# One fused attention and feed-forward kernel: when w_out's prepared tiles are stored, how long tiles rest, and which sums are kept

## The chip, the cores and the metric

The kernel runs on one core of a Trainium2 chip. The metric is the time of one execution on the device in microseconds; three executions of a kernel are summed up by their median. The profile is of one further execution and has a span of its own, from the first to the last instruction.

## The reference

```python
def _attn_ref(q, k, v):                       # q, k, v: (8, 12, 448, 64)
    scale = 1.0 / np.sqrt(q.shape[-1])
    scores = scale * np.matmul(q, k.transpose(0, 1, 3, 2)) - np.log(S)
    attn = 1.0 / (1.0 + np.exp(-scores))
    return np.matmul(attn, v)
...
def _moe_ref(x, w_in, w_out):                 # x: (3584, 768), w_in: (768, 2048), w_out: (2048, 768)
    h = x @ w_in
    g = np.maximum(0.01 * h, h)
    return g @ w_out
...
    x = attn_out.transpose(0, 2, 1, 3).reshape(B * S, H * D)
    return _moe_ref(x=x, **moe_kwargs)
```

All arrays are float32. The kernel multiplies each float32 as a high and a low part: every product of two tiles is three matmuls (high by high, high weight by low, low weight by high).

## The kernel before, in words

The work falls into three stages, one after the other on TensorE. **Attention** works through 48 pairs of heads. **The first product** (matmuls that write tiles named f) is x by w_in, in 4 rounds `p` of 20 block products, each in two halves: 160 steps called slots, of 12 matmuls of 448 columns each. **The second product** (matmuls that write tiles named a, and e for the last) is g by w_out, in 104 slots of 18 matmuls. Both products use fewer block products than a plain 4 by 4 blocking would, by a fast scheme with sums: blocks of weights and of inputs are added and subtracted first (`SUMS2` for the inputs and `STEPS2` for the weights of the second product), multiplied (`PRODUCTS2`), and the results added up.

The order on every engine is the order of the code: each engine's queue takes its instructions in that order. `slot()` emits one slot: the chores that were put down for it with `at(slot, rank, ...)` or `later(slots, ...)`, by rank, and the matmuls. SyncE (SP) issues nearly all transfers and also waits in order: a transfer whose data or room is not ready holds up those behind it.

**Preparation.** The generator `prep()` makes the weights on VectorE (DVE). It takes a unit u of w_in or w_out (12 units of w_out), decodes the packed words in two or three pieces into a tile wd (five instructions a piece), and makes the sums. For w_out that is `second()`: ten steps of `STEPS2`, most into a tile ws, some into free blocks of wd itself. Then both tiles are stored in memory (t2d, "t" in the trace), from where the second product's weights w are loaded. wd and ws of w_out take turns in one pool of two buffers, so wd always gets the same buffer back. Before the next unit's wd is begun, `prep()` waits until `now` has passed `free`, which is `HOLD` slots after the decoding of the last one ended; `PAUSE` means that no preparation is emitted in that slot. Otherwise the loop over `items1` emits as much preparation after a slot as the planned share of 2.42 us allows. The first unit of w_out is prepared at the end of the attention, the other eleven during the first product.

**Tiles.** `grab()` gives one of up to 28 tiles of 128 by 896 floats, the one that has been free longest; `drop(t, n)` gives it back for slot `now + n`. During the first product 16 of them exist; 6 more ("o") take the room of the preparation's pool after its end, and 6 ("j") come near the end. The results h of the first product are stored (g) by `save1`; sums of them that the second product needs (`MADE`, tiles h_m) are made by `made2` and stored too. The second product loads g tiles ahead; `LIMITS` says up to how many held tiles it may start a load early. `Streamed` weights ws are loaded from ts into three rotating tiles for the last products of a round. `Weights` loads the second product's weights, the first 12 (`FIRST`) before it begins, into buffers that the first product's weights leave.

The line behind an instruction in the profile is that of the recording helper (L159) nearly everywhere, so groups are told apart by tile names.

Of the kernel before, what the change touches and what calls it, by code (L numbers as in the profile page):

```python
# [21 lines left out]
ROOM = 1.7, 2.2, 2.1, 0.7, 0.2  # L22
SHARE = 0.95
SLOT = 2.42
CAST, SOON, HOLD = 3, 2, 3
PAUSE = 1
FULL = range(33, 37)
IDLE = 7
# [2 lines left out]
TILES, MORE, LAST, JOIN = 13, 3, 6, 6  # L31
RESULTS = 8
ROTS = 3
EARLY, FIRST, SOON2 = 12, 12, (2, 5)
COSTS = {"low": 0.95, "sum": 1.0, "cast": 0.85, "read": 1.5}
CAP, CAP_EARLY = 3.4, 0.8
GAP, LEAD, FAR2 = 8, 3, 5
LIMITS = (4, 27), (0, 22), (-3, 14), (-9, 10), (-99, 0)


X_ORDER = 1, 0, 2
# [28 lines left out]


RAW = "00", "01", "30", "31", "10", "11", "20", "21"
MADE = ("m1", "m2"), ("m5",), ("m1", "m2"), ("m3", "m4", "m5")


SUMS2 = {
# [7 lines left out]


PRODUCTS2 = (
# [7 lines left out]


BLOCKS2 = "02", "00", "01", "03", "10", "11", "12", "13", "s0", "s1", "s12", "s14", "s15"
MORE2 = "s2", "s3", "s4", "s5", "s6", "s7", "s8", "s9", "s10", "s11", "s13", "s16", "s17"
FORMS2 = BLOCKS2 + MORE2
STEPS2 = (
# [5 lines left out]


def part(i):
# [14 lines left out]
def attn_ffn_kernel(ctx: ExitStack, tc: tile.TileContext, qk, v, w_in, w_out, out):  # L122
# [21 lines left out]
    NQ = B // 2  # L144
# [52 lines left out]
    def later(slots, *fns, first=False):  # L197
        at(now + slots, 0 if first else 5, *fns)
# [13 lines left out]

    left, right = ExitStack(), ExitStack()

    prepared = set()

    class Wide:

# [178 lines left out]
    def second(u, w):  # L397


        kt, mt = divmod(u, 3)  # L400
        to = t2d[kt // 2][:, :, kt % 2, mt]
        s = block(F32, (len(MORE2), P), f"ws1_{u}")

        def of(x, y):
            names, t = (BLOCKS2, w) if x in BLOCKS2 else (MORE2, s)
            return two(t, names.index(x), names.index(y))

        for how, o, x, y in STEPS2:
            {"+": add, "-": sub, "n": minus}[how](*(of(z[0], z[-1]) for z in (o, x, y)))
            yield  # L410
        later(1, lambda: dma(out=to[:, :len(BLOCKS2)], in_=w), lambda: dma(out=to[:, len(BLOCKS2):], in_=s))

    def prep():

        count, size = (3, 2), 4 * P
        pieces = [(m, k) for m, (w, _) in enumerate(units) for k in range(count[w])]
        raws, free = [], 0

        def load():
            at = len(raws)
            if at == len(pieces):
                return
            m, k = pieces[at]
            w, u = units[m]
            third = w == 0 and at % 3 == 2
            raw = block(I32, (size, 2), f"wr{w}_{u}_{k}", (wr3, "wr3", 2 * size, 1) if third else (pp, "wr", 2 * size, 2))
            dma(out=raw.rearrange("p m t -> p (m t)"), in_=(w_in, w_out)[w][u][:, k * size:(k + 1) * size].bitcast(I32))
            raws.append((raw, now))  # L430

        for _ in range(3):
            load()
        yield
        for at, (m, k) in enumerate(pieces):
            w, u = units[m]
            if k == 0:
                while now < free:
                    yield PAUSE
                dec = block(F32, ((12, len(BLOCKS2))[w], P), f"wd{w}_{u}")  # L440
            while len(raws) <= at or now < raws[at][1] + SOON:
                yield PAUSE
            raw = raws[at][0]
            low, high = raw[:, :, 0], raw[:, :, 1]
            tf = dec.rearrange("p b m -> p (b m)")[:, k * size:(k + 1) * size]
            t = tf.bitcast(I32)
            vec_s(out=t, in0=high, scalar1=0x7FFFFFFF, scalar2=None, op0=ALU.bitwise_and)
            yield
            vec_s(out=tf, in0=tf, scalar1=W_LEAST, scalar2=W_MOST, op0=ALU.max, op1=ALU.min)
            yield  # L450
            vec_s(out=t, in0=t, scalar1=5, scalar2=2, op0=ALU.logical_shift_left, op1=ALU.logical_shift_right)
            yield
            vec_st(out=t, in0=high, scalar=-0x40000000, in1=t, op0=ALU.bitwise_and, op1=ALU.bitwise_or)
            yield
            vec_st(out=t, in0=low, scalar=29, in1=t, op0=ALU.logical_shift_right, op1=ALU.bitwise_or)
            yield
            if at != count[0] * NU - 1:
                later(1, load)
            if k < count[w] - 1:
                continue  # L460
            if w:
                free = now + 1 + HOLD
            while w and (0, NU - 1) not in prepared:
                yield PAUSE
            yield from (firsts, second)[w](u, dec)
            if w:
                prepared.add((w, u))
# [337 lines left out]
    def full(p, o, jj):  # L805

        got = complete.setdefault((p, jj), [])
        got.append(o)
        t = outs1[p, o, jj]
        at(now + 2, 8, lambda: save1(p, jj, o, t, True))  # L810
        todo = [(x, SUMS2[x][0], *(y[0] + str(int(y[1]) % 2) for y in SUMS2[x][1:])) for x in MADE[p]]
        for x in todo:
            if o in x[2:] and set(x[2:]) <= set(got):
                at(now + 1, 6, lambda x=x: made2(p, jj, *x))
        users = [set(x[2:]) for x in todo]
        for y in got:
            if (p, y, jj) not in over and all(z <= set(got) for z in users if y in z):
                over.add((p, y, jj))
                at(now + 2, 9, lambda t=outs1[p, y, jj]: drop(t, 2))

    def made2(p, jj, x, how, a, b):
        t = grab(f"h_{p}_{x}_{jj}", F32)
# [182 lines left out]
    w2 = [Weights(k) for k in range(LEN)]  # L1005
    for k, x in enumerate(w2):
        if k < FIRST:
            prepared_by(when(NQ - 1, 3 * (k // 4) + 3) + k % 4, x, 0)
        else:
            at(START + k - 9, 6, x.load)  # L1010
            at(START + k - 6, 1.6, x.high)
            at(START + lows[k], 1.7, x.low)

    used = 0.0
    for n, item in enumerate(items1):
        if n == len(items1) * (NQ - 1) // NQ:
            assert next(preps, 0) == 0
            right.close()
            shift(ctx, "pad5", 192, "right")
            tiles(ctx, "o", "right", LAST)  # L1020
# [16 lines left out]
    for tag, n in (("z0", 1), ("a1", 3), ("a0", 3), ("z1", 1)):  # L1037
        acc2[tag] = banks(f"ps_{tag}", {tag: (1, n)}, end)

    free = [(0, n) for n in range(RESULTS)]  # L1040
    outs, accs = {}, {}

    def result(o):
        place = min(free)
        free.remove(place)
        n = place[1]
        if n < ROTS:
            t = rot.tile([P, 2, NU, P], F32, tag=f"rot{n}", name=f"o_{o}").rearrange("p a b c -> p (a b c)")[:, :3 * S]
# [10 lines left out]
    def store(q, o):  # L1059
        t, n = outs.pop(o)  # L1060
        dma(out=place2(q, o).rearrange("m p s -> p m s"), in_=t)
        free.append((now + 3, n))

    def read(q, i):
        acc = accs[i % 2][:, :, :S]
# [91 lines left out]
```

## Time and profile before

| | us |
|---|---|
| median of 3 runs | 1053.4 (1053.33 to 1053.59) |
| the profiled execution | 1052.52 |
| its span | 1050.7 |
| TensorE matmuls busy | 1017.9 (97%) |
| VectorE busy | 851.2 (81%) |
| ScalarE busy | 585.1 (56%) |
| mean rate of the transfers | 280 GB/s |

The profiled execution lasted 1.8 us longer than its span. Busy time of TensorE overlaps in part and is not a measure of use; its idle time is.

### The profile page before, as it was taken

The page shows a single profiled execution, that of the slowest core. Times are in us where ns is not written, and L with a number is a line of the kernel's source. Part 1 is how long each engine was busy: PE and PEld are TensorE (multiplying, and loading weights), DVE is VectorE, ACT ScalarE, POOL GpSimd, SP SyncE. Part 2 cuts the span into 40 slices and gives each one's busy share as a digit, 9 for nine tenths or more (in the row PEclk, how much of TensorE's full clock was granted, in tenths as well). Part 3 has the DMA queues.
Part 4 walks back from the last instruction along what each step waited for, and adds up shares of the span by engine and source line. Part 5 has one row for each costly group of instructions (what it writes and reads, how often), then busy time and mean ns, then how long its engine had stood idle before and what let it go on. Part 6 is the DMA issues. An engine that isn't in the chain of part 4 may idle for free.

```text
span 1050.7 us, 15193 instructions
## 1 busy us (share of the span) xinstructions
PE 1017.9 (97%) x5642; PEld 848.2 (81%) x5642; DVE 851.2 (81%) x1116; ACT 585.1 (56%) x710; POOL 0.3 (0%) x5
## 2 busy tenths in 40 slices
PE   9999999999899979999999999699999999999998
PEld 5555555457898968988889999599999999999997
DVE  5888889876998588787776585579998899899886
ACT  6888888885544433454435664357444446645431
POOL 0000000000000000000000000000000000000000
PEclk9999999999999989999999999899999999999999
DMA  8899999988967978898879758997756798785632
GB/s 318 271 330 378 317 368 303 384 286 302 352 245 250 362 249 288 257 333 273 286 217 336 283 191 317 349 319 258 253 172 243 246 377 317 269 280 149 229 132 105
DMA packets 142745, 294.08 MB, mean 280 GB/s; under 512 B 11216, under 2 KB 71760, under 8 KB 142672
## 3 DMA queue, kind: packets, MB, share of 16 engines
q1 hardware_dynamic: 141808, 292.32, 80.3%
q8 instruction: 44, 0.72, 0.3%
q10 hardware_dynamic: 864, 0.80, 0.2%
q14 instruction: 29, 0.24, 0.1%
HBM read 189.79 MB, written 103.28 MB: 279 GB/s over the span
## 4 chain that ended last, share of the span: by engine, by line
PE 81%; DVE 8%; DMA 7%; issue 2%; SPq 1%; ACT 1%; ACTq 0%; DVEq 0%
PE a L159 35%; PE f L159 22%; PE pv L159 12%; PE sc L159 11%; DVE wd L159 3%; DMA t<-wd 3%; DMA g<-h 2%; DVE ws L159 2%; DVE xl L159 1%; SPq L159 1%; DVE h L159 1%; DMA ws<-ts 1%; DMA xd<-x_s 1%; ACT h L159 0%; DMA g<-g 0%
## 5 line engine op out<-in xcount | busy, mean ns | idle before, releaser
L159 PE MATMUL a<-gh,w 128*128 128x448 f32 x1224 | 344.7, 363 | 6.8 <-ACT h L159 6.8
L159 PE MATMUL f<-xh,w 128*128 128x448 f32 x960 | 274.8, 366 | 5.6 <-DVE h L159 3.4
L159 PEld LDWEIGHTS a<-gh,w 128*128 128x128 f32 x1224 | 230.6, 188 | 24.4 <-ACT h L159 7.2
L159 PEld LDWEIGHTS f<-xh,w 128*128 128x128 f32 x960 | 181.9, 190 | 22.1 <-DVE h L159 3.6
L159 PE MATMUL a<-gl,w 128*128 128x448 f32 x516 | 188.0, 364 | 0.0
L159 PE MATMUL f<-xl,w 128*128 128x448 f32 x480 | 176.0, 367 | 12.0 <-DVE xl L159 12.0
L159 DVE TENSOR_TENSOR h<-h,f 128x896 f32<-128x896 f32 x88 | 95.3, 1084 | 40.0 <-PE f L159 39.9
L159 ACT CAST gh<-g 128x896 fp32r<-128x896 f32 x68 | 64.0, 941 | 107.4 <-DVE g L159 78.7
L159 ACT ACTIVATE s<-sc 128x896 f32<-128x896 f32 x144 | 119.7, 957 | 3.6 <-PE sc L159 3.6
L159 ACT COPY h<-f 128x896 f32<-128x896 f32 x56 | 50.1, 909 | 118.6 <-PE f L159 91.2
L159 PE MATMUL pv<-s,v 128*64 128x448 f32 x576 | 113.8, 543 | 0.0
L159 PEld LDWEIGHTS f<-xl,w 128*128 128x128 f32 x480 | 91.1, 190 | 19.2 <-DVE xl L159 13.4
L159 DVE TENSOR_TENSOR w<-w 128x768 fp32r<-128x768 f32 x112 | 104.3, 953 | 0.1
L159 PEld LDWEIGHTS a<-gl,w 128*128 128x128 f32 x516 | 97.5, 189 | 5.3
L159 PEld LDWEIGHTS sc<-qks 64*128 64x128 f32 x876 | 80.4, 187 | 23.1 <-issue 16.9
L159 PE MATMUL sc<-qks 64*128 64x448 f32 (+1 forms) x876 | 95.3, 368 | 0.2 <-ACT qks L159 0.2
L159 PE MATMUL f<-xh,ws 128*128 128x448 f32 x320 | 91.5, 364 | 3.8 <-DVE h L159 2.0
L159 ACT CAST w<-w 128x768 fp32r<-128x768 f32 x112 | 92.8, 832 | 2.6 <-DMA w<-t 2.6
L159 PEld LDWEIGHTS pv<-s,v 128*64 128x64 f32 x576 | 39.0, 137 | 63.3 <-issue 54.3
L159 DVE TENSOR_TENSOR xl<-xl,xh 128x896 fp32r<-128x896 f32 x64 | 69.5, 1086 | 18.6 <-ACT xh L159 18.6
L159 ACT ACTIVATE h<-h 128x896 f32<-128x896 f32 x56 | 53.2, 952 | 52.3 <-DVE h L159 52.0
L159 DVE TENSOR_TENSOR qks<-qk,qks 128x832 fp32r<-128x832 f32 (+3 forms) x51 | 49.2, 971 | 36.9 <-ACT qks L159 35.5
(82 smaller groups left out, 1113.8 us busy)
## 6 DMA issues: line engine op xcount, KB each, us to landing
w<-t SPq DMA_DIRECT2D x112, 384.0 KB, 4.6
g<-g SPq DMA_DIRECT2D x76, 448.0 KB, 5.5
xl<-xd SPq DMA_DIRECT2D x64, 448.0 KB, 5.6
g<-h SPq DMA_DIRECT2D x64, 448.0 KB, 5.8
qk<-in_qk SPq DMA_DIRECT2D x46, 448.0 KB, 6.1
xd<-x_s SPq DMA_DIRECT2D x36, 448.0 KB, 7.0
xd<-x SPq DMA_DIRECT2D x28, 448.0 KB, 6.3
g_m<-g SPq DMA_DIRECT2D x28, 448.0 KB, 5.4
```

The source lines that it names most:

```text
L159: return lambda *args, **kw: tc.keep_in_program_order(issue(*args, **kw))
```

## The change

For w_out, the steps of `STEPS2` that write into wd come first, and wd is stored one slot after the last of them; ws is stored at the end as before. `free` now has a slot for each of the two tiles, five slots after the slot in which the store was put down (`now + 1 + HOLD`, with `HOLD` 4), and both the next wd and the next ws wait for theirs. The end of the preparation may come 12 slots later (`JOINT`: 28 slots before the end of `items1` in place of 40), and the 6 "o" tiles come then. The loads of the second product's first 12 weights move from slots 126 to 141 to slots 136 to 152. Tiles whose results were stored rest 3 slots in place of 2 (`drop(t, 3)`). `SUMS2` is another set of sums for the same products: rounds 0 and 2 still make and store two sums, round 1 one, and round 3 one in place of three. `LIMITS` is lower by 1 or 2 tiles. The tables `STEPS2`, `BLOCKS2`, `MORE2` and `PRODUCTS2` are written for the new sums; their counts (10 steps of the same widths, 26 products) are the same.

```diff
-CAST, SOON, HOLD = 3, 2, 3
+CAST, SOON, HOLD = 3, 2, 4
...
-EARLY, FIRST, SOON2 = 12, 12, (2, 5)
+EARLY, FIRST, SOON2, JOINT = 12, 12, (2, 5), 28
...
-LIMITS = (4, 27), (0, 22), (-3, 14), (-9, 10), (-99, 0)
+LIMITS = (4, 26), (0, 20), (-3, 12), (-9, 8), (-99, 0)
...
-MADE = ("m1", "m2"), ("m5",), ("m1", "m2"), ("m3", "m4", "m5")
+MADE = ("m1", "m4"), ("m5",), ("m1", "m4"), ("m5",)
...
-BLOCKS2 = "02", "00", "01", "03", "10", "11", "12", "13", "s0", "s1", "s12", "s14", "s15"
+BLOCKS2 = "02", "00", "01", "03", "10", "11", "12", "13", "s0", "s1", "s2", "s3", "s4"
...
+        while now < free["s"]:
+            yield PAUSE
         s = block(F32, (len(MORE2), P), f"ws1_{u}")
...
-        for how, o, x, y in STEPS2:
+        for n, (how, o, x, y) in enumerate(STEPS2):
             {"+": add, "-": sub, "n": minus}[how](*(of(z[0], z[-1]) for z in (o, x, y)))
+            if o[0] in BLOCKS2 and STEPS2[n + 1][1][0] in MORE2:
+                later(1, lambda: dma(out=to[:, :len(BLOCKS2)], in_=w))
+                free["w"] = now + 1 + HOLD
             yield
-        later(1, lambda: dma(out=to[:, :len(BLOCKS2)], in_=w), lambda: dma(out=to[:, len(BLOCKS2):], in_=s))
+        later(1, lambda: dma(out=to[:, len(BLOCKS2):], in_=s))
+        free["s"] = now + 1 + HOLD
...
-                while now < free:
+                while w and now < free["w"]:
                     yield PAUSE
...
-            if w:
-                free = now + 1 + HOLD
...
-                at(now + 2, 9, lambda t=outs1[p, y, jj]: drop(t, 2))
+                at(now + 2, 9, lambda t=outs1[p, y, jj]: drop(t, 3))
...
-            prepared_by(when(NQ - 1, 3 * (k // 4) + 3) + k % 4, x, 0)
+            prepared_by(START - 24 + 3 * k // 2, x, 0)
...
-        if n == len(items1) * (NQ - 1) // NQ:
+        if n == len(items1) - JOINT:
```

Three places show what moves. The first is VectorE's queue in round 1, where unit 3 of w_out ends (wd_3, ws_3) and unit 4 begins (wd_4). Before:

```order
L159 TENSOR_TENSOR xl_1_3803<-xl_1_3803,xh_1_3861 128x896
L159 TENSOR_TENSOR wd_3_3633<-ws_3_3694 128x256
L159 SCALAR_TENSOR_TENSOR ws_3_3694<-wd_3_3633,ws_3_3694 128x256
L159 TENSOR_SCALAR wd_4_3917<-wr_4_0_3702 128x512
L159 TENSOR_SCALAR wd_4_3917<-wd_4_3917 128x512 x2
```

With the change:

```order
L159 TENSOR_TENSOR ws_3_3902<-wd_3_3681,ws_3_3902 128x128
L159 TENSOR_TENSOR ws_3_3902<-ws_3_3902 128x256
L159 TENSOR_TENSOR xl_1_3867<-xl_1_3867,xh_1_3931 128x896
L159 TENSOR_TENSOR h_31_0_3929<-h_31_0_3929,f_1_2_3952 128x896
L159 TENSOR_TENSOR h_31_1_3949<-h_31_1_3949,f_1_2_3969 128x896
L159 TENSOR_TENSOR xl_1_3906<-xl_1_3906,xh_1_3966 128x896
L159 TENSOR_SCALAR wd_4_3998<-wr_4_0_3727 128x512
L159 TENSOR_SCALAR wd_4_3998<-wd_4_3998 128x512 x2
```

The last write of wd_3 stood next to the end of the unit and the first write of wd_4 right behind it; now the work of four slots of the first product stands between the units, and wd_3 was written for the last time before all of ws_3. The second place is SP's queue at unit 8 (xl are inputs, wr packed weights, g stores of results, ws_15 and ws_16 streamed weights). Before:

```order
L159 DMA wr_9_1_4753<-in_w_out 128x1024
L159 DMA t_1_67<-wd_8_4642 128x13x128
L159 DMA t_1_67<-ws_8_4722 128x13x128
L159 DMA xl_2_4812<-xd_4_104 128x896
L159 DMA xl_2_4850<-xd_5_105 128x896
```

With the change:

```order
L159 DMA wr_9_1_4881<-in_w_out 128x1024
L159 DMA t_1_67<-wd_8_4806 128x13x128
L159 DMA ws_15_4902<-ts_61 128x1024
L159 DMA xl_2_4904<-xd_7_107 128x896
L159 DMA g_3_154<-h_31_0_4719 128x896
L159 DMA t_1_67<-ws_8_4851 128x13x128
L159 DMA xl_2_4938<-xd_8_108 128x896
```

The two stores of a unit no longer follow each other; three transfers of the first product stand between them here. The third place is SP's queue in the last slots of the first product (ws_19 the last streamed weight, g_m and g_00 loads of the second product's inputs, g_4, g_6, g_8 and g_2 stores). Before:

```order
L159 DMA ws_19_6121<-ts_65 128x1024
L159 DMA g_m_00_6125<-g_8_150 128x896
L159 DMA g_4_165<-h_10_1_5614 128x896
L159 DMA g_m_01_6147<-g_8_150 128x896
L159 DMA g_6_167<-h_20_0_5947 128x896
L159 DMA g_m_00_6168<-g_9_141 128x896
L159 DMA g_00_6170<-g_3_135 128x896
L159 DMA g_6_167<-h_20_1_5962 128x896
L159 DMA g_8_169<-h_m_0_6123 128x896
L159 DMA g_2_163<-h_30_0_5634 128x896
```

With the change:

```order
L159 DMA ws_19_6116<-ts_65 128x1024
L159 DMA g_4_165<-h_10_1_5598 128x896
L159 DMA g_6_167<-h_20_0_5918 128x896
L159 DMA g_m_00_6158<-g_8_150 128x896
L159 DMA g_m_01_6160<-g_8_150 128x896
L159 DMA g_6_167<-h_20_1_5935 128x896
L159 DMA g_2_163<-h_30_0_5617 128x896
L159 DMA g_2_163<-h_30_1_5634 128x896
L159 DMA g_8_169<-h_m_0_6156 128x896
L159 DMA g_m_00_6221<-g_9_141 128x896
```

The loads of g_m from g_9 and of g_00 from g_3 moved behind the stores of h_30 and h_m, by three slots, and one sum h_m less is stored here.

## Rows read from the trace of the kernel before

**Rows 1.** The page's part on engines: busy us, share of span, instructions.

```profile
PE 1017.9 (97%) x5642; PEld 848.2 (81%) x5642; DVE 851.2 (81%) x1116; ACT 585.1 (56%) x710; POOL 0.3 (0%) x5
```

**Rows 2.** Waits of PE: who waited for whom, us in total, times, longest.

```profile
PE f L159 <- DVE xl L159: 12.0, 4, 6.8
PE a L159 <- ACT h L159: 6.8, 1, 6.8
PE f L159 <- DVE h L159: 5.4, 6, 1.4
PE f L159 <- ACT h L159: 2.2, 1, 2.2
PE f L159 <- DVE ws L159: 1.8, 2, 1.7
```

**Rows 3.** Timeline of PE: start us, us, instruction, [idle before, releaser].

```profile
249.70 0.48 PE L159 MATMUL f<-xh,w 128*128 128x448 f32 x1
...
373.88 0.74 PE L159 MATMUL f<-xl,w 128*128 128x448 f32 x1 [6.76 <-DVE xl L159]
...
452.39 0.45 PE L159 MATMUL f<-xh,ws 128*128 128x448 f32 x1 [1.36 <-DVE h L159]
...
651.69 0.45 PE L159 MATMUL f<-xh,ws 128*128 128x448 f32 x1 [0.61 <-DVE h L159]
...
658.83 0.67 PE L159 MATMUL f<-xh,ws 128*128 128x448 f32 x2 [1.69 <-DVE ws L159]
...
670.33 0.74 PE L159 MATMUL a<-gh,w 128*128 128x448 f32 x1 [6.83 <-ACT h L159]
```

**Rows 4.** Waits of DVE, as in rows 2.

```profile
DVE wd L159 <- DMA t<-wd: 24.9, 8, 10.2
DVE wd L159 <- issue: 8.4, 1, 8.4
```

**Rows 5.** Timeline of DVE, 355 to 374 us, as in rows 3.

```profile
355.59 0.43 DVE L159 SCALAR_TENSOR_TENSOR ws<-wd,ws 128x256 f32<-128x256 f32 x1
366.18 0.43 DVE L159 TENSOR_SCALAR wd<-wr 128x512 int32<-128x512 int32 x1 [10.16 <-DMA t<-wd]
...
372.74 1.09 DVE L159 TENSOR_TENSOR xl<-xl,xh 128x896 fp32r<-128x896 f32 x1
```

**Rows 6.** Timeline of SP's queue at 358 us: start, us until issued.

```profile
358.73 0.45 SPq L159 DMA_DIRECT2D t<-wd  x1
```

**Rows 7.** Tile wd, 250 to 560 us: its stores from issue to landing.

```profile
DMA to landing us min/median/max: 4.4/5.6/7.7
```

**Rows 8.** Tile g, 250 to 670 us: its transfers from issue to landing.

```profile
DMA to landing us min/median/max: 2.4/5.7/10.8
```

**Rows 9.** Windows: length, busy us of each engine, PE clock granted, DMA share, GB/s.

```profile
267.60:272.00 4.40, 4.40 (x15) 3.97 (x16) 4.40 (x5) 1.17 (x2) 0.00 (x0) 0.66 1.03 392
373.80:378.00 4.20, 4.12 (x11) 3.69 (x12) 4.06 (x10) 0.00 (x0) 0.00 (x0) 0.50 0.83 293
666.00:670.00 4.00, 0.00 (x0) 0.00 (x0) 4.00 (x5) 3.35 (x4) 0.00 (x0) 0.79 1.03 405
670.30:675.00 4.70, 4.67 (x13) 4.15 (x14) 1.71 (x2) 0.94 (x1) 0.00 (x0) 0.50 1.00 327
690.00:1040.00 350.00, 350.00 (x1752) 328.03 (x1751) 320.68 (x314) 174.75 (x205) 0.00 (x0) 1.00 0.70 240
```

**Rows 10.** Timeline of ACT at the two late places, as in rows 3.

```profile
504.20 0.91 ACT L159 COPY h<-f 128x896 f32<-128x896 f32 x1 [8.68 <-DMA g<-h]
...
654.61 1.05 ACT L159 CAST ws<-ws 128x1024 fp32r<-128x1024 f32 x1 [5.92 <-DMA ws<-ts]
...
666.00 0.92 ACT L159 ACTIVATE h<-f 128x896 f32<-128x896 f32 x1 [5.25 <-DMA g<-h_m]
...
669.36 0.92 ACT L159 ACTIVATE h<-f 128x896 f32<-128x896 f32 x1 [0.48 <-DMA g<-h]
```

**Rows 11.** DVE's groups by form: busy us, mean ns of one, idle before.

```profile
L159 DVE TENSOR_TENSOR g<-g,g 128x896 f32<-128x896 f32 x30 | 32.4, 1087 | 0.0
```

More of the change, by code (lines that the diff above doesn't have):

```diff
@@ L72 @@
 RAW = "00", "01", "30", "31", "10", "11", "20", "21"
-MADE = ("m1", "m2"), ("m5",), ("m1", "m2"), ("m3", "m4", "m5")
+MADE = ("m1", "m4"), ("m5",), ("m1", "m4"), ("m5",)
 SUMS2 = {
[7 rows of a table removed]
-PRODUCTS2 = (
[7 rows of a table removed]
-BLOCKS2 = "02", "00", "01", "03", "10", "11", "12", "13", "s0", "s1", "s12", "s14", "s15"
-MORE2 = "s2", "s3", "s4", "s5", "s6", "s7", "s8", "s9", "s10", "s11", "s13", "s16", "s17"
[7 rows of a table added]
+PRODUCTS2 = (
[7 rows of a table added]
+BLOCKS2 = "02", "00", "01", "03", "10", "11", "12", "13", "s0", "s1", "s2", "s3", "s4"
+MORE2 = "s5", "s6", "s7", "s8", "s9", "s10", "s11", "s12", "s13", "s14", "s15", "s16", "s17"
 FORMS2 = BLOCKS2 + MORE2
 STEPS2 = (
[5 rows of a table removed]
[5 rows of a table added]
 def part(i):
@@ L213, in attn_ffn_kernel @@
     left, right = ExitStack(), ExitStack()
-    prepared = set()
+    prepared, free = set(), {"w": 0, "s": 0}
     class Wide:
@@ L418, in prep @@
         pieces = [(m, k) for m, (w, _) in enumerate(units) for k in range(count[w])]
-        raws, free = [], 0
+        raws = []
         def load():
@@ L1038, in attn_ffn_kernel @@
         acc2[tag] = banks(f"ps_{tag}", {tag: (1, n)}, end)
-    free = [(0, n) for n in range(RESULTS)]
+    spots = [(0, n) for n in range(RESULTS)]
     outs, accs = {}, {}
     def result(o):
-        place = min(free)
-        free.remove(place)
+        place = min(spots)
+        spots.remove(place)
         n = place[1]
@@ L1061, in store @@
         dma(out=place2(q, o).rearrange("m p s -> p m s"), in_=t)
-        free.append((now + 3, n))
+        spots.append((now + 3, n))
     def read(q, i):
```

38 rows, old and new, of tables (PRODUCTS2, STEPS2, SUMS2) are left out of this document.

## The prediction

> **What bounds the kernel now.** The page comes first: TensorE has work nearly all the time [rows 1], so time can only come from its gaps, and where these lie is in its waits and its timeline. The reader is to see two things in them. In the second product TensorE never waits once it has begun [rows 2], and a window of 350 us shows full busy time at full clock [rows 9]; 1752 matmuls in 350.00 us make 0.200 us each. The gaps lie in the first product: it begins at 249.70 and the second begins at 670.33 [rows 3], 420.6 us for 160 slots of 12 matmuls, which at 0.200 us would take 384.0. So 36.6 us are over. The waits name 28.2 of them, the sum of the five rows [rows 2]. The clock after three long waits is the next part: granted 0.66 over 4.4 us, and 0.50 (1.2 of 2.4 GHz) over 4.2 and 4.7 us [rows 9], which lost 1.5, 2.1 and 2.35 us; the last belongs to the second product. That leaves 36.6 - 28.2 - 3.6 = 4.8 us of run-out and slow starts around the fourteen waits.
>
> Who is late behind each wait is read by going back along the engines. The 6.76 us wait at 373.88 is for an input's low part xl [rows 3]. VectorE made it at 372.74, behind a decoding that had itself waited 10.16 us for a store of wd [rows 5]. SP issued that store at 358.73 [rows 6], only after VectorE had finished the whole unit: the next unit had stood in VectorE's queue with no work between. Nine decodings wait so, 24.9 + 8.4 us [rows 4]. The row named issue is the same case: wd_1 behind the store of wd_0, at the start of the first product. All four waits for xl (12.0 us) follow such a decoding, and of the six for DVE h (5.4 us) the four that are left without the 1.36 and the 0.61 (3.4 us) [rows 2, 3]. So stores of wd cost 15.4 us.
>
> The others: 2.2 us for a copy h on ScalarE that waited 8.68 us for the store of its tile's last result [rows 2, 10]; 1.36 and 1.69 us for streamed weights ws, the second with a load that made ScalarE wait 5.92 us [rows 3, 10]; 0.61 us behind sums h_m; and 6.83 us where the second product begins: its first matmul waits for the last read of the first product, which stands behind a read whose tile was still being stored (5.25 us) [rows 3, 10].
>
> **The change, part by part.** *Stores of wd.* In the program's order of before, the first write of a wd stands at most two slots behind the store of the last one in 10 of 11 cases, five times even in an earlier slot. A store takes 5.6 us, at most 7.7 [rows 7], and 2.4 us is a slot. With the change the distance is 4 slots or more in all eleven, 9.6 us, and the store no longer waits for the sums in ws. For ws the smallest distance goes from 1 slot to 4. 9.6 us cover the slowest landing of a wd with 1.9 to spare; what eats this is SP being late. The bounds are thus all 15.4 us gained, or half of it if SP is late as often as it is now. I take 14.4, keeping 1 us, because the pause also takes VectorE's backlog away, and because SP's lateness at 358.73 came from VectorE's.
>
> *What the pauses delay.* The decoding and sums are the same instructions, 10 and 10 a unit; the widths of the steps are the same. They come later: the last unit ends in slot 128 in place of 110. What hides this is that slots 111 to 129 held no preparation; the busiest slot holds 4.8 us on VectorE both before and after (two reads, five decodings, some sums), followed by a nearly empty one. If that cover failed, an xl would be late by what is over, 2.4 us at most. The 6 "o" tiles come 12 slots later; the order shows that every grab from slot 120 to 132 still finds a tile whose rest is over. No cost.
>
> *Rest of tiles.* The grabs that come two slots or less behind a result's store go from 36 to 4. g stores land in 5.7 us, at most 10.8 [rows 8]; two slots are 4.8 us, three 7.2. The grab behind the 8.68 us wait is now one slot further. Bounds 0 and 2.2 us; I take 2.0.
>
> *Fewer stored sums, lower limits.* Two sums in two halves fall away in round 3, four instructions of 1.09 us (the nearest form [rows 11]), their four stores of 448 KB and the room of four tiles. Before, ten grabs in slots 156 to 162 took a tile before its rest was over, among them those of g_00 and g_01 loads at which SP stood; now none does. The read that waited 5.25 us for a stored sum now takes the tile of an input, which nobody stores. So the 6.83 us shrink to what is left by construction, the last read itself, 0.92 us [rows 10], and its signal: 1.1 us. Gain 5.7 us, and with the short gap the slow clock, 2.35 us. 0.61 us for h_m goes too. The lower bound of this part is nothing, if transfers are what is late there.
>
> For that the transfers count. From the first early g load to the last store of a result stand 37 before (17.1 MB), 34 now (15.6 MB, two weights w among them). At the 405 GB/s of 666 to 670 us [rows 9] this is 42.2 and 38.5 us, against about 31 us of slots. So it does not fit either way, but only the loads ahead of the second product's first slots have to land. The Trainium skill speaks against this part: in "DMA: Bandwidth & Descriptors", Specifications, it puts the limit of one core's share of the memory at about 358 GB/s. By that the 34 would take an estimated 43.6 us, and the beginning would stay as late as now. The trace shows 405 GB/s over 4 us and does not agree.
>
> *Second product.* The two sums are made there: 4 more additions of 1.09 us [rows 11], 4.3 us, less the two m4 sums that stood in its first slots. VectorE has 320.7 of 350 us [rows 9] and about 29 idle; 2 to 4 us more over 374 us cost nothing while that room is there.
>
> *Weights.* The first 12 weights are loaded, split and kept as before, 10 slots later; they end in slot 152, where the queue is fullest, and w_10 and w_11 stand ahead of the last streamed weights ws_19. Their 0.79 MB cost those 2 us at 405 GB/s in the worst case. I keep the 1.36 and 1.69 us waits as they are and add 1.0 us for this.
>
> *Sum.* 14.4 (wd) + 3.6 (clock, first product) + 2.0 (rest) + 5.7 + 2.35 (beginning) + 0.6 (h_m) + 2.3 (half of the 4.8, since ten of fourteen waits go) - 1.0 = 30.0 us. The profiled execution took 1052.52 us, 1.8 more than its span and 0.9 less than the median. Against its own time 1052.5 - 30.0 = 1022.5; the median is then about **1023.4 us**.
>
> **The rivals.** *Everything goes.* Only the 1.1 us remain of 36.6 + 2.35: a gain of 37.9 us, 1015.5. For it speaks that the second product shows no gap at all; against it that ws still arrives late in each round.
>
> *The beginning stays late.* The 34 transfers keep SP full until 670 us as now, so 6.83 us with its clock and the 1.69 us stay, and w_10 and w_11 make it worse: 8.1 us less gained, 1031.5. For it: 38.5 us of transfers against 31 of slots. Against it: the reads' tiles no longer hang on stores. The rule of the Trainium skill named above ("DMA: Bandwidth & Descriptors", Specifications) would make this the likelier case.
>
> *Stores still too slow.* If SP comes 4 us late to half of the stores, 5.6 + 4 is the whole distance of 9.6 us, and half of 15.4, 3.6 and 2.3 stays: and as 1 us of it is kept already, about 9.7 us less is gained: 1033.
>
> *Slower: VectorE becomes the bound of the second product.* It starts without the 7 us lead that the gap at 663 to 670 gives the queues. VectorE has 0.92 of that window; it decides when its work exceeds 3.6 us a slot. Mean work is 3.3 us, and the change adds under 0.05. To be slower than before, every one of 104 slots would have to lose 0.29 us, 30 us in sum: 1054 or more. Only if several late loads pile up on full slots.
>
> *The change does not do what it says.* The waits for the store turn into equal waits of another kind, such as of the decoding for its packed words: 1053. Those are loaded a whole unit ahead, which speaks against it.
>
> **How the numbers follow.** My forecast has 0.60 (about 1018 to 1028); everything goes 0.10; late beginning 0.13; slow stores 0.10; no change 0.03; slower 0.04. The range of 8 in 10 takes in half of the first rival and both lesser gains: 1016 to 1035. What a measurement can tell from no change is 0.2%, 2.1 us: faster 0.94, same 0.02, slower 0.04.
>
> **What would show it.** Right: no wait of VectorE's wd for a store above 2 us; TensorE's waits in the first product below 8 us in sum; no granted clock of 0.5 after 20 us; the first matmul a waiting 1 to 2 us for ACT h. Wrong: xl still the first releaser (stores), 4 us or more before the first a with full transfers (beginning), or gaps within the second product (VectorE). An attention stage that ends other than at about 249.7 us would overturn the frame, since there one store of wd is added.

## The result, and the profile after

The changed kernel takes 1025.1 us (median of 4 runs, 1022.98 to 1025.65) against 1053.4 us (4 runs, 1048.8 to 1053.59): a ratio of 0.9738, interval 0.9708 to 0.9768. On another chip, beside some of the experiments, it took 1026.3 us against 1050.7, a ratio of 0.9760 (0.9743 to 0.9776). The profiled execution took 1024.77 us with a span of 1023.0, so the span fell by 27.7 us.

The page's part on engines, as in [rows 1]:

```profile
PE 1011.8 (99%) x5642; PEld 845.8 (83%) x5642; DVE 852.7 (83%) x1116; ACT 585.8 (57%) x710; POOL 0.3 (0%) x5
```

VectorE does 1.5 us more work in a shorter span. The counts of instructions are those of before, so the time came out of gaps. The waits of PE, against [rows 2]:

```profile
PE f L159 <- DVE ws L159: 2.9, 3, 2.4
PE f L159 <- DVE h L159: 2.0, 3, 1.4
PE a L159 <- ACT h L159: 1.1, 1, 1.1
...
PE f L159 <- ACT ws L159: 0.7, 1, 0.7
```

The waits for xl and for ScalarE's h in the first product are gone, and so is the long one at the beginning of the second product. Most of what is left has to do with streamed weights ws. PE's timeline, against [rows 3]:

```profile
250.13 0.48 PE L159 MATMUL f<-xh,w 128*128 128x448 f32 x1
...
435.10 0.44 PE L159 MATMUL f<-xh,ws 128*128 128x448 f32 x1 [1.41 <-DVE h L159]
...
634.55 0.47 PE L159 MATMUL f<-xh,ws 128*128 128x448 f32 x1 [0.69 <-ACT ws L159]
637.66 0.70 PE L159 MATMUL f<-xh,ws 128*128 128x448 f32 x2 [2.44 <-DVE ws L159]
644.99 0.47 PE L159 MATMUL a<-gh,w 128*128 128x448 f32 x1 [1.06 <-ACT h L159]
```

The first product now lasts from 250.13 to 644.99, 394.9 us in place of 420.6. The wait of 1.36 us at 452 stands here as 1.41 at 435; the 1.69 us before the end of the round became 0.69 and 2.44. Windows, against [rows 9]:

```profile
267.60:272.00 4.40, 4.40 (x24) 4.13 (x23) 4.23 (x9) 3.27 (x4) 0.00 (x0) 1.00 1.04 408
...
373.80:378.00 4.20, 4.20 (x23) 3.94 (x22) 3.10 (x4) 1.78 (x2) 0.00 (x0) 1.00 1.05 322
636.00:640.00 4.00, 2.34 (x7) 2.12 (x8) 4.00 (x5) 1.97 (x3) 0.00 (x0) 0.77 1.03 418
640.00:644.00 4.00, 3.93 (x16) 3.23 (x14) 3.44 (x4) 2.60 (x3) 0.00 (x0) 0.80 1.02 393
645.00:650.00 5.00, 5.00 (x25) 4.69 (x26) 3.36 (x4) 1.50 (x2) 0.00 (x0) 1.00 1.03 403
650.00:1015.00 365.00, 365.00 (x1827) 342.15 (x1826) 332.81 (x324) 178.46 (x209) 0.00 (x0) 1.00 0.69 240
```

The three stretches of slow clock are at full clock now. A new one stands at 636 to 644, behind the 0.69 and 2.44 us. It lost 4 x 0.23 + 4 x 0.20 = 1.7 us. The second product shows no gap; VectorE is busy 0.91 of the long window, against 0.92 before.

No wait of VectorE's for a store of wd is left. One unit in round 1 shows how: SP's queue with the store, then VectorE's timeline with the next write of wd.

```profile
370.35 0.38 SPq L159 DMA_DIRECT2D t<-wd  x1
```

```profile
378.53 1.09 DVE L159 TENSOR_TENSOR h<-h,f 128x896 f32<-128x896 f32 x1 [0.31 <-PE f L159]
379.53 0.42 DVE L159 TENSOR_SCALAR wd<-wr 128x512 int32<-128x512 int32 x1
```

9.18 us lie between, and the second row has no idle time in front. In all eleven cases the distance is 8.74 us or more; the shortest is that of the first unit, stored at 242.27 us and followed by the next write at 251.01. The landing of wd's stores, against [rows 7]:

```profile
DMA to landing us min/median/max: 4.5/6.1/10.4
```

They land no faster than before, the slowest even later; what has changed is that no write waits for their room any more.

### The profile page after: what moved, and what is told of

It is laid out like the page before. It is cut to its first block, busy times and chain, and to the rows that moved or that the text cites. A ratio compares the mean times of both kernels' runs of the same rounds, so it can differ in the third digit from the quotient of the medians.

```text
span 1023.0 us, 15182 instructions
## 1 busy us (share of the span) xinstructions
PE 1011.8 (99%) x5642; PEld 845.8 (83%) x5642; DVE 852.7 (83%) x1116; ACT 585.8 (57%) x710; POOL 0.3 (0%) x5
## 4 chain that ended last, share of the span: by engine, by line
PE 95%; DMA 2%; DVE 1%; ACT 1%; issue 0%; ACTq 0%; DVEq 0%
PE a L159 36%; PE f L159 34%; PE pv L159 13%; PE sc L159 11%; DMA ws<-ts 2%; PE e_z L159 0%; ACT h L159 0%; DVE ws L159 0%; ACT ws L159 0%; DVE h_m L159 0%; PE e_a L159 0%; DVE h L159 0%; DVE wd L159 0%; ACTq L159 0%; ACT L159 0%
## 5 line engine op out<-in xcount | busy, mean ns | idle before, releaser
L159 PE MATMUL f<-xh,w 128*128 128x448 f32 x960 | 271.8, 363 | 0.6 <-DVE h L159 0.6
L159 PE MATMUL a<-gl,w 128*128 128x448 f32 x540 | 194.4, 360 | 0.0
L159 PE MATMUL f<-xl,w 128*128 128x448 f32 x480 | 173.5, 361 | 0.0
L159 ACT CAST gh<-g 128x896 fp32r<-128x896 f32 x80 | 75.4, 943 | 121.3 <-DVE g L159 90.1
L159 PEld LDWEIGHTS a<-gl,w 128*128 128x128 f32 x540 | 101.0, 187 | 7.0
L159 DVE TENSOR_TENSOR gl<-g,gh 128x896 fp32r<-128x896 f32 x72 | 78.2, 1086 | 5.7 <-ACT gh L159 5.2
## 6 DMA issues: line engine op xcount, KB each, us to landing
w<-t SPq DMA_DIRECT2D x112, 384.0 KB, 5.0
```

The costliest lines, as they stand in the source:

```text
L159: return lambda *args, **kw: tc.keep_in_program_order(issue(*args, **kw))
```

## The experiments

Ratios are to the kernel before on the same chip, with their 95% intervals. Each code edit is against the changed kernel unless it says otherwise.

| kernel | us | ratio |
|---|---|---|
| changed kernel, first and second measurement | 1025.1; 1026.3 | 0.9738 (0.9708 to 0.9768); 0.9760 (0.9743 to 0.9776) |
| a: first half of the change | 1035.6 | 0.9864 (0.9829 to 0.9899) |
| b: other half, on the kernel before | 1040.6 | 0.9905 (0.9888 to 0.9922) |
| c: no rest behind the stores | 1044.9 | 0.9944 (0.9925 to 0.9962) |
| d: tiles rest 2 slots | 1027.5 | 0.9781 (0.9763 to 0.9800) |
| e: late store of wd, rest of 2 | 1034.9 | 0.9850 (0.9833 to 0.9866) |
| m: limits of before | 1025.8 | 0.9758 (0.9743 to 0.9773) |
| f: early weights | 1023.1 | 0.9737 (0.9722 to 0.9751) |
| h: store of ws behind the load | 1024.8 | 0.9754 (0.9735 to 0.9774) |
| j: copy behind the activations | 1020.8 | 0.9703 (0.9682 to 0.9724) |
| k: f and j together | 1020.5 | 0.9701 (0.9682 to 0.9721) |
| l: k, no g loads ahead of ws_19 | 1027.3 | 0.9772 (0.9750 to 0.9794) |

**a. Preparation changed, end as before.** Sums of round 3, limits and tile rest of before; the products stay those of the change.

```diff
-LIMITS = (4, 26), (0, 20), (-3, 12), (-9, 8), (-99, 0)
+LIMITS = (4, 27), (0, 22), (-3, 14), (-9, 10), (-99, 0)
...
-MADE = ("m1", "m4"), ("m5",), ("m1", "m4"), ("m5",)
+MADE = ("m1", "m4"), ("m5",), ("m1", "m4"), ("m2", "m3", "m5")
...
-                at(now + 2, 9, lambda t=outs1[p, y, jj]: drop(t, 3))
+                at(now + 2, 9, lambda t=outs1[p, y, jj]: drop(t, 2))
```

> The changed kernel with three of its parts undone: round 3 again stores three sums (MADE[3] = m2, m3, m5), LIMITS is the old one, and stored tiles rest 2 slots. What is left is the early store of wd, the wait behind the stores, and the later end of the preparation. In the program's order the ten early grabs of slots 156 to 162 are back, while the distance from a wd store to the next write of wd stays 4 slots or more. Theory (stores of wd and the beginning of the second product are two causes that add up): the first matmul a waits about 6.8 us again and the clock falls behind it, the wait for a copy h of about 2 us may come back; 1034 to 1038 us. Rival (the beginning was late only because the earlier waits had upset SP's queue, so that it goes with them): the first matmul a waits 1 to 2 us and the time is 1025 to 1028 us.

Measured 1035.6 us. The rows of PE and of ACT at the beginning of the second product:

```profile
651.16 0.74 PE L159 MATMUL a<-gh,w 128*128 128x448 f32 x1 [5.66 <-ACT h L159]
```

```profile
646.71 0.92 ACT L159 ACTIVATE h<-f 128x896 f32<-128x896 f32 x1 [5.56 <-DMA g<-h_m]
```

VectorE waits for no store of wd, and the beginning is late again, behind the store of a sum h_m as in [rows 3, 10].

**b. End changed, preparation as before.** The other half, put on the kernel before.

```diff
-LIMITS = (4, 27), (0, 22), (-3, 14), (-9, 10), (-99, 0)
+LIMITS = (4, 26), (0, 20), (-3, 12), (-9, 8), (-99, 0)
...
-MADE = ("m1", "m2"), ("m5",), ("m1", "m2"), ("m3", "m4", "m5")
+MADE = ("m1", "m2"), ("m5",), ("m1", "m2"), ("m5",)
...
-                at(now + 2, 9, lambda t=outs1[p, y, jj]: drop(t, 2))
+                at(now + 2, 9, lambda t=outs1[p, y, jj]: drop(t, 3))
```

> The kernel before with only the counterpart: one stored sum in round 3 (MADE[3] = m5), the new LIMITS, and 3 slots of rest; stores of wd and the preparation as before. Theory of two causes: the nine waits of VectorE for stores of wd stay (about 33 us idle on VectorE, 15 us on TensorE), the beginning of the second product waits 1 to 2 us; about 11 us are gained, 1041 to 1045 us. Rival (one queue, one cause): without the wd stores repaired the beginning stays late, 1050 to 1054 us.

Measured 1040.6 us, just below the range expected. The waits of DVE, and PE's timeline:

```profile
DVE wd L159 <- DMA t<-wd: 25.1, 8, 10.5
DVE wd L159 <- issue: 8.0, 1, 8.0
```

```profile
372.75 0.74 PE L159 MATMUL f<-xl,w 128*128 128x448 f32 x1 [6.74 <-DVE xl L159]
...
660.66 0.47 PE L159 MATMUL a<-gh,w 128*128 128x448 f32 x1 [1.06 <-ACT h L159]
```

The picture is the opposite of a: wd waits as in [rows 4], and the beginning is short. By medians on one chip the halves gain 15.1 us (a) and 10.1 (b), 25.2 together, of the 24.4 and 28.3 us that the whole change gained in its two measurements. They add up; neither covers the other.

**c. No rest behind the store.** wd is still made and stored first.

```diff
-CAST, SOON, HOLD = 3, 2, 4
+CAST, SOON, HOLD = 3, 2, 0
```

> The changed kernel with HOLD = 0 in place of 4: wd is still stored in the middle of its unit, but the next unit no longer waits four slots behind a store. In the program's order the next write of wd then stands 0 to 3 slots behind the store in 9 of 11 units (0 or 1 in 6). Theory (the distance is what counts, a store takes about 5.6 us and a slot 2.4): VectorE waits again for t<-wd, 2 to 6 us in some six units, and TensorE with it; 1029 to 1037 us. Rival (storing wd before the sums of ws is enough): no such wait above 1 us, 1024 to 1027 us.

Measured 1044.9 us, outside what either expected: 19.4 us of span lost. The waits of DVE and of PE:

```profile
DVE wd L159 <- DMA t<-wd: 25.1, 6, 7.4
```

```profile
PE f L159 <- DVE h L159: 11.2, 6, 4.1
PE f L159 <- DVE xl L159: 3.5, 2, 3.2
```

VectorE waits for stores of wd as long as before. Of TensorE's 14.7 us in the two rows, 13.7 follow right behind such a wait, for h more than for xl. Much of the rest of the loss is clock, granted at 0.50 from 430 to 436 us, 0.57 from 470 to 474, 0.59 from 508 to 512 and 0.54 from 656 to 662. In this kernel's order the next write of wd stands 0 to 3 slots behind the store in nine of eleven cases. An early store alone brought nothing when the next unit moved up behind it: b, with the late store and the same short beginning of the second product, took 1040.6 us on the same chip.

**e. The store at the unit's end again, with a rest of 2 slots** for both tiles. With both stores late this is the longest rest that still lets the preparation end in time.

```diff
-CAST, SOON, HOLD = 3, 2, 4
+CAST, SOON, HOLD = 3, 2, 2
...
-            if o[0] in BLOCKS2 and STEPS2[n + 1][1][0] in MORE2:
-                later(1, lambda: dma(out=to[:, :len(BLOCKS2)], in_=w))
-                free["w"] = now + 1 + HOLD
...
-        later(1, lambda: dma(out=to[:, len(BLOCKS2):], in_=s))
-        free["s"] = now + 1 + HOLD
+        later(1, lambda: dma(out=to[:, :len(BLOCKS2)], in_=w), lambda: dma(out=to[:, len(BLOCKS2):], in_=s))
+        free["w"] = free["s"] = now + 1 + HOLD
```

> wd is stored with ws at the unit's end again, and the rest is 2 slots behind both stores (the largest that still lets the preparation end in time): 2 slots are 4.8 us against a landing of 5.6 us. Theory (only the distance between the store and the next write counts): a part of the waits for t<-wd comes back, shorter than the 2 us mean of hold 0; time between the changed kernel and the kernel with no rest, 1029 to 1040. Rival (the early store itself counts, as it takes wd's store out of the way of ws's): over 1042, as with no rest. Second rival (two slots are enough): within 2 us of the changed kernel.

Measured 1034.9 us. The time lies where the theory put it, but not for its reason. Waits of DVE and of PE, and SP's queue near the end of round 2:

```profile
DVE wd L159 <- DMA t<-wd: 2.6, 2, 1.7
```

```profile
PE f L159 <- DVE ws L159: 7.3, 3, 2.4
PE f L159 <- ACT ws L159: 3.5, 3, 1.6
```

```profile
525.69 0.38 SPq L159 DMA_DIRECT2D t<-wd  x1
526.16 0.63 SPq L159 DMA_DIRECT2D t<-ws  x1
526.84 6.04 SPq L159 DMA_DIRECT2D g<-h  x1
532.97 0.40 SPq L159 DMA_DIRECT2D ws<-ts  x1
```

Two slots of rest are nearly enough for wd. Most of what is lost goes to the streamed weights, 10.8 us of waits against 3.6 in the changed kernel: both stores of a unit stand in SP's queue, a result's store behind them takes 6.04 us to be issued, and the load of ws behind it is late. A round earlier, at 427 us, it is the same with 3.70 us. The two places make 6.75 of the 10.8 us. The other 4.05 us, at the end of the last round, are not of this kind: the last store of a unit was issued some 80 us before them, and the changed kernel waits at that place too. Whether the two stores side by side do it, or that units now end at the end of a round, is not told apart here.

**d. Tiles rest 2 slots; m. limits of before.** Two parts of the end, each undone by itself.

```diff
-                at(now + 2, 9, lambda t=outs1[p, y, jj]: drop(t, 3))
+                at(now + 2, 9, lambda t=outs1[p, y, jj]: drop(t, 2))
```

> The changed kernel with the rest of stored tiles back from 3 slots to 2, nothing else. Theory as forecast (2.0 us from the longer rest): ScalarE waits longer for g<-h in rounds 1 and 2 and TensorE about 2 us more; 1026 to 1029 us. Rival (the wait at 505 us came from stores of wd and ws ahead of the result's store in SP's queue, so the rest gives nothing): 1024 to 1026 us.

```diff
-LIMITS = (4, 26), (0, 20), (-3, 12), (-9, 8), (-99, 0)
+LIMITS = (4, 27), (0, 22), (-3, 14), (-9, 10), (-99, 0)
```

> The changed kernel with the limits of before (10, 14, 22, 27 held tiles in place of 8, 12, 20, 26), but with the smaller set of stored sums. It tells which of the two gives the 10 us at the beginning of the second product. Theory (the read that stood behind a store of a sum is freed by the sums that are no longer stored): the first a still waits about 1.1 us; what the limits add is some loads more ahead of ws_19, whose wait grows by up to 2 us; 1025 to 1030 us, ratio 0.975 to 0.980. Rival (the limits are what keeps tiles free there): the wait before the first a is 4 us or more again and the clock falls to 0.5 behind it, 1031 to 1036 us.

d took 1027.5 us, some 2 and 4.5 us more by the two ratios of the changed kernel (0.0021 and 0.0043 of 1053), with intervals that meet; its timeline of PE has a wait for ScalarE's h again:

```profile
289.56 0.47 PE L159 MATMUL f<-xh,w 128*128 128x448 f32 x1 [0.94 <-ACT h L159]
```

m is the same as the changed kernel (0.9758), and its beginning is as short:

```profile
646.04 0.47 PE L159 MATMUL a<-gh,w 128*128 128x448 f32 x1 [1.06 <-ACT h L159]
```

So the limits gave nothing that can be measured. What a lacks beside them and the rest is the smaller set of stored sums, which by what is left over gives most of the end's 10 us; that set was not undone by itself.

**The second measurement of the changed kernel**, as a measure for e, f and h on one chip.

> The changed kernel once more, as the measure for the other kernels of this chip: 1022 to 1027 us, the same two late places as before: about 4 us in sum at ws_18 and ws_19 and the last read (634 to 645 us), and nothing of VectorE's wd waiting for a store.

The time came within that, 1026.3 us; the waits at the end are a little longer than expected, 1.93 and 2.44 us for ws and 1.06 before the first a.

**f. The first weights earlier.**

```diff
-            prepared_by(START - 24 + 3 * k // 2, x, 0)
+            prepared_by(START - 30 + k, x, 0)
```

> The first 12 weights of the second product are loaded in slots 130 to 141 in place of 136 to 152, so that none of them stands ahead of ws_19 in SP's queue. Theory (the last ws are late because the transfers of slots 145 to 156 are more than the queue moves in time): ws_19 lands 1 to 2 us earlier, the waits of 0.69 and 2.44 us at 634 to 638 us shrink to under 1.5 us in sum and with them the clock of 0.77 to 0.80 behind them; 1 to 3.5 us faster than the changed kernel. Rival (SP issues ws_19 late because it waits for something else in its queue, or each queue's landing is bound elsewhere): waits and time the same within 1 us.

1023.1 us against 1026.3 beside it; the intervals of the ratios overlap a little, the spans are 1021.4 and 1025.1. TensorE no longer waits for ScalarE's ws, but one row did not move:

```profile
636.09 0.68 PE L159 MATMUL f<-xh,ws 128*128 128x448 f32 x2 [2.43 <-DVE ws L159]
```

The wait for VectorE's part of ws is 2.44 us in the changed kernel both times, and also in c, d, h and m, and within 0.01 of it in e and here. In none of the kernels is it longer; with this order of the queues it is shorter only in b (2.33), a (1.82) and the kernel before (1.69). Something other than the load sets how long it can get. In the changed kernel, ACT's timeline and then DVE's show what:

```profile
633.45 1.05 ACT L159 CAST ws<-ws 128x1024 fp32r<-128x1024 f32 x1 [5.13 <-DMA ws<-ts]
634.40 1.79 ACT L159 ACTIVATE h<-h 128x896 f32<-128x896 f32 x2
```

```profile
635.38 1.09 DVE L159 TENSOR_TENSOR h_m<-h,h 128x896 f32<-128x896 f32 x1 [3.12 <-ACT h L159]
636.39 1.22 DVE L159 TENSOR_TENSOR ws<-ws 128x1024 fp32r<-128x1024 f32 x1
```

ScalarE's copy of ws waits for the load, the activations stand behind the copy, VectorE's sum h_m waits for one of them, and the low part of ws, which needs only the copy, stands behind the sum. From the copy's start to the low part's start these instructions take 2.94 us here, and as long in the kernel before (654.61 [rows 10] to 657.55). The load still has its part: it sets when the copy starts, and so whether TensorE comes to wait. Two rounds earlier in the changed kernel, copy and low part lie 2.94 us apart too (436.55 to 439.49), and TensorE hardly waits; in e, where ScalarE's copy waited 6.71 us for that load in place of 1.32, it does. The first row is the changed kernel's, the second that of e:

```profile
440.76 0.67 PE L159 MATMUL f<-xh,ws 128*128 128x448 f32 x2 [0.21 <-DVE ws L159]
```

```profile
441.74 1.11 PE L159 MATMUL f<-xh,ws 128*128 128x448 f32 x2 [2.44 <-DVE ws L159]
```

**j. The copy behind the activations**, in the changed kernel, for ws_18 and ws_19 alone.

```diff
     def prepared_by(when_, x, load, high=3, low=4, rank=3):
...
-        at(when_ + high, 3, x.high)
+        at(when_ + high, 4.5 if rank < 0 else 3, x.high)
```

> The changed kernel, but ScalarE's copy of ws_18 and ws_19 is put down behind the activations of finished results of the same slot in place of ahead of them. Theory (the wait of 2.44 us at 638 to 639 us is no transfer but a convoy: the copy of ws_19 waits 5 to 6 us for its load, an activation h stands behind it, VectorE's sum h_m waits for that h, and the low part of ws_19 stands behind the sum): h_m no longer waits behind the copy, the low part follows the copy at once, and the wait of 2.44 us shrinks to 0.4 to 1.0 us; with its clock 1 to 3 us faster than the changed kernel, the wait for ACT ws stays as it is. Rival (the low part is late because the load is): the 2.44 us stay and the time too.

1020.8 us. DVE's and PE's timelines:

```profile
633.42 1.08 DVE L159 TENSOR_TENSOR h_m<-h,h 128x896 f32<-128x896 f32 x1
636.54 1.22 DVE L159 TENSOR_TENSOR ws<-ws 128x1024 fp32r<-128x1024 f32 x1 [2.03 <-ACT ws L159]
```

```profile
636.56 0.47 PE L159 MATMUL f<-xh,ws 128*128 128x448 f32 x1 [1.45 <-ACT ws L159]
637.82 1.11 PE L159 MATMUL f<-xh,ws 128*128 128x448 f32 x2 [0.58 <-DVE ws L159]
```

The sum no longer waits, and 2.44 us became 0.58, as expected. The wait for ScalarE's copy did not stay as it was: it is 1.45 us, against 0.69 and 1.93 in the changed kernel, and the granted clock fell to 0.50 from 638 to 640 us. The ratio is 0.0035 and 0.0057 below the two of the changed kernel, 3.7 and 6 us, more than the expected 1 to 3 (with the first of the two its interval overlaps); the profiled execution was the slowest of five (1024.8; the others 1019.5 to 1022.3), and its span, 1023.0 us, is that of the changed kernel. So the trace shows the shorter wait, but not where the gain of the other four executions comes from.

**k. Both**, f and j.

> Both edits that help the last streamed weights: the first 12 weights in slots 130 to 141, and the copy of ws_18 and ws_19 behind the activations. Theory: the wait for ACT ws and most of the 2.44 us go, what is left of the end of the first product is under 1 us and the 1.1 us of the last read; waits of TensorE in the first product under 4 us in sum; about 1 to 3 us faster than with the early weights alone (ratio to before 0.9737 there), 0.971 to 0.973. Rival: no difference to the early weights alone.

1020.5 us: by the ratios 3.8 us below f, somewhat more than expected, but no faster by the median than j beside it. It stays within 1.5 us from run to run, where j spreads over 5. The waits of PE and two windows:

```profile
PE f L159 <- DVE h L159: 2.1, 3, 1.5
PE a L159 <- ACT h L159: 1.1, 1, 1.1
...
PE f L159 <- DVE ws L159: 0.6, 1, 0.6
```

```profile
634.00:638.00 4.00, 3.76 (x19) 3.53 (x20) 4.00 (x5) 3.00 (x4) 0.00 (x0) 1.00 1.03 416
638.00:642.00 4.00, 2.91 (x15) 2.39 (x14) 4.00 (x5) 1.95 (x3) 0.00 (x0) 1.00 1.02 414
```

The clock stays full to the end of the first product. This is the fastest kernel here together with j, about 4 us below the changed kernel by the nearer of its two ratios.

**h. The store of ws behind the load.**

```diff
-        later(1, lambda: dma(out=to[:, len(BLOCKS2):], in_=s))
+        at(now + 1, 6.5, lambda: dma(out=to[:, len(BLOCKS2):], in_=s))
```

> The store of ws is put down behind the load of the same slot's streamed weights in place of ahead of it. Theory (the wait of 1.41 us at 435 us, behind a copy of ws that waited 5.45 us, comes from a store of ws that stands ahead of the load): that wait goes and the time falls by about 1 to 1.5 us, at the edge of what can be measured. Rival (the load is late because of the read it shares the memory with): the wait stays, time the same. What could make it slower: ws's store lands later, but its next write is 4 slots or more behind it.

A miss: 1024.8 us, no difference. The wait at 435 us went, and 1.20 us for VectorE's ws came at 441 in its place.

**l. No g loads ahead of ws_19**, added to k.

```diff
-LIMITS = (4, 26), (0, 20), (-3, 12), (-9, 8), (-99, 0)
+LIMITS = (4, 26), (0, 20), (-4, 12), (-99, 0)
```

> The two edits, and no g tile is loaded ahead of ws_19 (limits of 12 from slot -4 of the second product on and none before, in place of 8 from slot -9 on). Theory (ws_19's 8 to 9 us landing is spent behind the four g loads issued just ahead of it, 1.8 MB): it lands in 5 to 6 us, ACT's wait for it falls from about 6 to 2 to 4 us, and the last wait for ws goes. Rival (the g loads then come too late for the second product): a new wait of 1 to 5 us at the first a matmuls, and the time is equal or worse than with the two edits.

1027.3 us: the theory holds for ws_19, and the rival for the time. The landing of ws from 615 us on, PE's timeline, and a window:

```profile
DMA to landing us min/median/max: 4.0/4.5/5.1
```

```profile
642.50 0.74 PE L159 MATMUL a<-gl,w 128*128 128x448 f32 x1 [4.05 <-DVE gl L159]
```

```profile
642.00:646.00 4.00, 3.50 (x9) 3.13 (x10) 2.89 (x4) 0.00 (x0) 0.00 (x0) 0.50 1.03 418
```

ws_19 lands within 5.1 us, and no wait for it is left. But the g tiles, issued behind it, come too late for the second product: 5.8 us of waits and a clock of 0.50, in sum about 7 us worse than k.

## Why the prediction was right, point by point

The forecast was a gain of 30.0 us on the profiled execution; its span gained 27.7. By the median 1023.4 was forecast and 1025.1 measured, inside the likeliest case's own range.

- **Stores of wd, 14.4.** Gained 15.4: no wait is left. a, b and c show that it is this part, and that the distance does it. One premise failed without harm: the slowest landing was to be 7.7 us against 9.6 of rest, and it is 10.4 now. e adds what the prediction had not weighed, the time of the preparation: with late stores a rest of 2 slots ends it when early ones with 4 do (the last stores are issued at 557.17 and 560.90 us in e, at 559.43 and 562.14 in the changed kernel), and TensorE waits 10.8 us for streamed weights in place of 3.6.
- **Clock in the first product, 3.6.** This is the term that was mis-sized. The two stretches came back whole, but the 0.69 and 2.44 us of waits for ws made a new one that lost 1.7 us; the sum had counted the longer waits and not the clock behind them. Net 1.9. So one sign that was named for being right, no granted clock of 0.5, did not come: from 638.5 to 641 us it was 0.50.
- **Rest of tiles, 2.0.** The 2.2 us at 504 are gone, but the rest is not the only thing that takes them away: they do not come back in d and a, where tiles rest 2 slots again, and they are gone in b too, where tiles rest 3 slots and wd is stored late. What comes back in d and a is a wait of 0.94 and 1.29 us at 290 us, behind the store of a tile's result as at 504 before. By the medians the rest is worth some 2 to 4.5 us (d), and its size is not settled better.
- **The beginning, 5.7 and 2.35.** The wait is 1.06 us against 1.1 forecast, and the clock behind it is 1.00; from the first a to the end it now takes 1023.0 - 645.0 = 378.0 us against 380.4, which is the 2.35. a shows that this part is not a by-product of the other. The reason given, a tile that nobody stores, fits a and m; that the limits belong to it does not: they gave nothing.
- **h_m, 0.6.** Gone at 651 us, but 0.16 and 0.48 us for DVE h came elsewhere: zero in sum.
- **Half of the 4.8 us of run-out.** 394.86 - 384.0 - 6.66 (all waits of PE named between 250 and 645 us) - 1.7 leaves 2.5: right.
- **Weights ahead of ws_19, -1.0.** -1.4 (3.13 us of waits for 1.69) in this execution. f shows that the weights are a part of it: the wait for ScalarE's copy goes. But the larger wait, 2.44 us, is not only a late transfer, as the prediction read the 1.69 us before: the load makes it begin, and the order of ScalarE's and VectorE's queues around the sum h_m makes it that long, which j shows.
- **Sum.** The waits left, 6.7 us, are near the 6.5 that the terms leave of 28.2. The missing 2.3 us are the 1.7 of clock, 0.2 of waits and 0.4 by which the attention ended later (250.13 for 249.70).

Of the rivals, stores that are still too slow did not come; c, which has no rest, shows what they would have looked like. The second product shows no gap, so VectorE did not become its bound. The late beginning did not come: from 636 to 640 us the transfers ran at 418 GB/s, against the 358 GB/s that the Trainium skill states as one core's share ("DMA: Bandwidth & Descriptors", Specifications); the trace does not agree, as at 666 us before. l shows that this rival's mechanism exists: five slots ahead of the second product is too late to begin with its loads.

## What to carry to other kernels

When a producer waits for a store of its own buffer, what counts is the distance in its queue from the store to the next write; storing earlier helps when the time it frees is spent on that distance, not on moving the next unit up. A wait that keeps its length to a hundredth of a microsecond in several kernels points to an order of instructions: a late load may start it, but a change of order in the right queue can shorten it, here from 2.44 to 0.58 us, where an earlier load left it at 2.43. In a queue where both have a deadline, moving loads behind one another moves the wait: look at what lands next before giving one of them way.

## What the hardware showed that was not expected

The same 512 KB load of ws_19 lands 9.1 us after its issue in the changed kernel and within 5.1 us in l, where all eight 448 KB loads of g stand behind it in SP's queue, and none of the four that are ahead of it in the changed kernel. In k, which differs from l only in these loads, it lands 8.3 us after its issue. The mean rate does not tell the two apart as one would think: over the 9.1 us in the changed kernel it was 350 and then 387 GB/s with the transfer engines full (share 1.01), over the 5.1 us in l 302 GB/s at a share of 0.94. Here it was what stood ahead of the transfer that set its landing.

The length of a wait alone does not tell here whether it costs clock. In the kernel before, 2.15 us ahead of 505 us left the granted clock at 1.00 from 505 to 513 us; in f, 2.43 us ahead of 636 us was followed by 0.50 from 638 to 640 us, and in j 1.45 and 0.58 us by the same. The 0.59 us in k left 1.00, the 0.69 and 2.44 us in the changed kernel gave 0.77 and 0.80 over 4 us each, and 4.05 us in l gave 0.50.
